# Linear attention and two feed-forward layers: a step's matmuls regrouped by array shape, scores of two heads in turn, decay tables pair by pair

## The chip, the cores and the metric

One core of a Trainium2 chip runs the whole kernel. The metric is the device time of one execution in microseconds (us). TensorE (PE; its weight loads are PEld), VectorE (DVE), ScalarE (ACT) and GpSimd (POOL) work beside each other; SyncE (SP) issues the loads. An engine works through its instructions in the order in which the program issues them, and waits on semaphores for what other engines make.

## The reference

Three layers in a row, all float32:

```python
# attention: q, k, v (4, 8, 768, 64), lam (8,); blocks of 64
for b in range(nb):
    intra = einsum('bhic,bhjc->bhij', qb, kb) * Dmask      # lam ** (i - j), i >= j
    intra = einsum('bhij,bhjd->bhid', intra, vb)
    inter = einsum('bhid,bhde->bhie', qb * lam_pow, kv_state)
    out[:, :, sl] = intra + inter
    kv_state = lam_block * kv_state + einsum('bhsd,bhse->bhde', kb * rev_pow, vb)
# soft mixture of 8 experts on x = out as (3072, 512)
logits = x @ phi                                            # 32 slots
slot_input = softmax(logits, axis=0).T @ x
slot_out[e] = relu(slot_input[e] @ w1[e]) @ w2[e]
x = softmax(logits, axis=1) @ slot_out
# feed-forward: 512 -> 2048 -> 512
h = x @ w_in
return (h * sigmoid(1.702 * h)) @ w_out                     # w_in, w_out stored as float64
```

## The kernel before, in words

The kernel works in blocks of 128 positions (chunks), not 64. A half sequence of one batch (384 positions, R = 3 chunks) is a group `g`, of which there are NG = 8; a group has NHP = 4 pairs of heads. One group and one pair is a step `s`, so there are NSTEP = 32. Two heads of 64 columns lie side by side in 128 partitions.

A step's work is cut into functions, and a loop written out by hand (L524 to L597) runs them for several steps at once: iteration `i` runs the scores of step i+1, the transposes of step i+2, the output of step i and the output transposes of step i-1. This order is the order of the instructions on every engine; nothing reorders it. The parts:

- `load_step` (L111): loads of q, k and v by SP into rotating buffers; a load waits until its buffer is free.
- `do_q` (L240): ScalarE turns the loaded q into the order by chunks.
- `do_T` (L247): TensorE transposes q and k (128x128, three chunks each), ScalarE copies them out as qT and kT.
- `do_SC` (L283): scores, k against q, one head after the other, three chunks each. A head uses 64 rows of the array, the other head the other 64, and each has its PSUM bank ("s0", "s1"). VectorE multiplies each head's scores with its decay table `dec` into AT. With `between`, which step 0 uses, the transposes of step 1 stand between the heads.
- `do_kd` (L275): ScalarE scales k by the decay to the end of the chunk. `do_qd` (L269): GpSimd scales qT.
- `do_ST` (L299): per chunk and head one 128x64 matmul of kd and v into bank "st", then VectorE updates the states (two instructions of 64x64 per chunk).
- `do_X` (L320): the output of a step in bank "x": the state part (one 128x128 matmul per chunk, L328; the very first chunk of a sequence has none) and the attention part, v against AT (128x64, per chunk and head; L332 for the very first chunk, L337 for the others). ScalarE copies it out as xT.
- `do_XT` (L342): three 128x128 transposes of xT into bank "xt", copied out by ScalarE as x in natural order.

Every four steps a group's tail runs, in pieces spread over iterations by `ph` = i mod 4: `tail_logits` (128x32 matmuls with phi, bank "m"), `tail_L` (transposes, then reductions on VectorE), `tail_max` (running maximum), `tail_exp` (the maximum broadcast by a small matmul on 32 rows, then exponentials), and one group later `tail_slot`, `tail_acc`, `tail_z` (128x32 matmuls of the exponentials with x into bank "xt" and with ones into bank "m"; VectorE adds both up).

An fp32 matmul appears in the trace as two records, a transpose as one.

Ahead of the loop VectorE makes the eight decay tables (`make_dec`, L492, a scan of 128x128 per head) and the powers `qtab`. Weights of the experts come in 64 pieces of 512 KB (`load_pieces`, `load_piece`), 33 of them during the steps, nine as the attention's rooms come free, the rest as experts free theirs; ten float64 pieces of w_in and w_out are loaded and converted early as well. After the steps come the last group's tail, the experts (L775 on) and the feed-forward part (L1049 on).

Of the kernel before, what the change touches and what calls it, by code (L numbers as in the profile page):

```python
# [17 lines left out]
def attention_moe_gelu_kernel(  # L18
# [16 lines left out]
    B, H, S, D = q.shape  # L35
# [44 lines left out]
    def bank(tag, name):  # L80
        return psp.tile([P, 512], F32, tag=tag, name=name)
# [149 lines left out]
    def state(s, c):  # L231

        b, hf, hp, g = step_of(s)
        if c == R:
            return S_3[hp]
        return S_a[2 * (s % 2) + (c - 1 if c < R else c - R - 1)]
# [10 lines left out]
    def do_T(s):  # L247
        b, hf, hp, g = step_of(s)
        qt, kt = q_t[s], k_t[s]
        bq = bank("tq", "bq")  # L250
        bk = bank("tk", "bk")
        for c in range(R):
            PE.transpose(bq[:, c * P:(c + 1) * P], qt[:, c].rearrange("p h d -> p (h d)"), ident)  # L253
        for c in range(R):
            PE.transpose(bk[:, c * P:(c + 1) * P], kt[:, c].rearrange("p h d -> p (h d)"), ident)  # L255
        def room(tag, elsewhere):
            if elsewhere:
                return tailp.tile([P, HS], F32, tag="xT", name=tag, bufs=NHP + 1)
            return early.tile([P, HS], F32, tag=tag, name=tag, bufs=1)


        t = room("qT", s in (1, NSTEP - 1))
        ACT.activation(out=t.rearrange("m (p c) -> m c p", c=R), in_=bq[:, :HS].rearrange("m (c p) -> m c p", c=R),  # L263
                       func=AF.Copy)
        tk = room("kT", s == 1)
        ACT.activation(out=tk, in_=bk[:, :HS], func=AF.Copy)
        qT[s], kT[s] = t, tk
# [12 lines left out]
                           scale=dec[:, 2 * hp + h, P - 1:P])  # L280
        kd[s] = t

    def do_SC(s, between=None):  # L283
        b, hf, hp, g = step_of(s)
        bs = [bank(f"s{h}", "bs") for h in range(2)]
        for h in range(2):
            if h == 1 and between:
                between()
            hs = slice(h * D, (h + 1) * D)
            for c in range(R):  # L290
                cs = slice(c * P, (c + 1) * P)
                PE.matmul(bs[h][:, cs], kT[s][hs, cs], qT[s][hs, cs], start=True, stop=True)  # L292
        for h in range(2):
            t = attn.tile([P, R, P], F32, tag=f"AT{h}", name="AT")
            DVE.tensor_tensor(out=t, in0=bs[h][:, :HS].rearrange("m (c i) -> m c i", c=R),  # L295
                              in1=dec[:, 2 * hp + h, None, :].to_broadcast([P, R, P]), op=ALU.mult)
            AT[s, h] = t
# [19 lines left out]
                                             scalar=qtab[r, hp, P - 1:P], in1=src,  # L317
                                             op0=ALU.mult, op1=ALU.add)

    def do_X(s):  # L320
        b, hf, hp, g = step_of(s)
        bx = bank("x", "bx")


        first = hf * R
        for c in range(R):
            if first + c > 0:
                PE.matmul(bx[:, c * P:(c + 1) * P], state(s, first + c), qdT[s][:, c, :],  # L328
                          start=(first > 0 and c == 0), stop=False)
            else:  # L330
                for h in range(2):
                    PE.matmul(bx[h * D:(h + 1) * D, 0:P], v_t[s][:, 0, h, :], AT[s, h][:, 0, :],  # L332
                              start=True, stop=False)
        for c in range(R):
            if first + c > 0:
                for h in range(2):
                    PE.matmul(bx[h * D:(h + 1) * D, c * P:(c + 1) * P], v_t[s][:, c, h, :],  # L337
                              AT[s, h][:, c, :], start=False, stop=(c == R - 1))
        xT[s] = tailp.tile([P, HS], F32, tag="xT", name="xT", bufs=NHP + 1)
        ACT.activation(out=xT[s], in_=bx[:, :HS], func=AF.Copy)  # L340

# [71 lines left out]

    def tail_exp(g, tag="m", between=None, room="e"):
        bb = bank(tag, "bb")
        PE.matmul(bb[:, :NS], mr[g % 2][:NS].to_broadcast([NS, P]), ident[:NS, :NS], start=True, stop=True)
        a = tailp.tile([P, R, NS], F32, tag="a", name="a", bufs=1)
        DVE.tensor_tensor(out=a, in0=tl["L", g], in1=bb[:, None, :NS].to_broadcast([P, R, NS]), op=ALU.subtract)
        if between:
            between()  # L420
        e = tailp.tile([P, R, NS], F32, tag=room, name="e", bufs=1)
        ACT.activation(out=e, in_=a, func=AF.Exp)
        if g > 0:
            ACT.activation(out=tl["al", g], in_=tl["md", g], func=AF.Exp)
        tl["e", g] = e
# [46 lines left out]
    with tc.manual_schedule():  # L472
# [7 lines left out]
        def warm_up(n):  # L480
            for _ in range(n):
                PE.matmul(bwarm, warm[:, :P], warm, start=True, stop=True)
# [9 lines left out]
        def make_dec(h):  # L492

            DVE.tensor_tensor_scan(out=dec[:, h], data0=lam_b[:, h:h + 1].to_broadcast([P, P]), data1=ident,
                                   initial=0.0, op0=ALU.mult, op1=ALU.add)
# [5 lines left out]
        while n < P:  # L501
            DVE.tensor_tensor(out=qtab[:, :, n:2 * n], in0=qtab[:, :, 0:n],
                              in1=qtab[:, :, n - 1:n].to_broadcast([P, NHP, n]), op=ALU.mult)
            n *= 2
        for h in range(2, H):
            make_dec(h)
        load_step(1, "v")
        load_step(2, "q")
        for t in S_a + S_3:
# [3 lines left out]
        def make_isum():  # L513
            for j in range(G):
                for i in range(G):
                    POOL.tensor_copy(out=isum4[i * NS:(i + 1) * NS, j, :],
                                     in_=ident[i * NS:(i + 1) * NS, i * NS:(i + 1) * NS])
# [6 lines left out]
        for i in range(-2, NSTEP):  # L524
            g, ph = divmod(i, NHP)
            if i > -2:
                load_step(i + 4, "q")
            if i == 1:
                make_isum()
            if 0 <= i + 1 < NSTEP:  # L530

                do_SC(i + 1, (lambda: do_T(1)) if i == -1 else None)
            if 0 <= i + 2 < NSTEP:
                if i != -1:
                    do_T(i + 2)
                if i == -2:
                    warm_up(1)
                do_q(i + 3)
            if ph == 0 and 0 <= g - 2 < NG:
                tail_slot(g - 2)  # L540
                tail_acc(g - 2)
                tail_z(g - 2)
            if ph == 2 and 0 <= g - 1 < NG and i < NSTEP - 2:
                tail_max(g - 1)
            if ph == 3 and 0 <= g - 1 < NG:
                tail_exp(g - 1)
            if 0 <= i + 1 < NSTEP:
                do_ST(i + 1)
            if 0 <= i + 2 < NSTEP:
                do_kd(i + 2)  # L550
            if 0 <= i < NSTEP:
                if i == NSTEP - 1:
                    tail_logits_first(NG - 1)
                if i == NSTEP - 2:
                    tail_max(g - 1)
                do_X(i)
            if i == NSTEP - 4:
                load_pieces(i + 1)
            if i >= 0:
                load_step(i + 3, "v")  # L560
            if 0 <= i + 2 < NSTEP:
                do_qd(i + 2)
            load_step(i + 4, "k")
            if i == -2:
                load_step(2, "v")
                SP.dma_start(out=phi_sb, in_=phi.rearrange("(k p) s -> p k s", p=P))
            load_pieces(i)
            if 0 <= i - 1 < NSTEP:
                do_XT(i - 1)
            c, turn = divmod(i - 2, EVERY)  # L570
            if turn == 0 and 0 <= c < len(EARLY):
                do_early(c)
            if turn == 0 and 0 <= c + 1 < len(EARLY):
                load_early(c + 1)
            if ph == 0 and 0 <= g - 1 < NG:
                tail_logits(g - 1)
            if ph == 1 and 0 <= g - 1 < NG:
                tail_L(g - 1)
            if ph == 3 and 0 <= g - 1 < NG and i < NSTEP - 1:
                tail_row(g - 1)  # L580
            if ph == 0 and 0 <= g - 2 < NG:
                tail_row_exp(g - 2)
            if i == NSTEP - 2:
                early_cm.__exit__(None, None, None)
                slotb_cm = tc.tile_pool(name="slotb", bufs=NPC_B, side="right", reuse_waits="tile")
                slotb = slotb_cm.__enter__()

                rooms = [piece_room(NPC + j) for j in reversed(range(NPC_B))]
                while rooms:
                    load_piece(rooms.pop())  # L590
            if i == NSTEP - 1:
                attn_cm.__exit__(None, None, None)
                slotc_cm = tc.tile_pool(name="slotc", bufs=NPC_C, side="left", reuse_waits="tile")
                slotc = slotc_cm.__enter__()
                for _ in range(NPC_C):
                    load_piece()
# [495 lines left out]
```

## Time and profile before

| what | value |
|---|---|
| time, median of 3 runs | 526.29 us (526.19 to 527.05) |
| the profiled execution | 527.16 us, of which the span of instructions is 525.1 us |
| PE / PEld busy | 510.4 us (97%) / 390.5 us (74%) |
| DVE / ACT / POOL busy | 273.6 (52%) / 276.9 (53%) / 62.5 us (12%) |
| mean granted TensorE clock | 0.996 |
| moved by DMA | 76.18 MB |

The span has three parts: the attention steps up to about 171 us, the last tail and the experts up to about 214 us, and the feed-forward part. A matmul's record lasts longer than the distance to the next, since matmuls are pipelined; what a group costs is therefore read from its first start to the first start of the next group. "128*64" after an operation is the part of the array in rows and columns. The DMA share is the time that packets took, summed, over 16 engines; packets on one engine overlap a little, so it can pass 1.

### The profile page before, as it was taken

To read this page: it belongs to the slowest core of one execution; us is meant where nothing else is said; L and a number is where in the kernel's file an instruction comes from. 1 tells how busy PE (TensorE), PEld (TensorE's weight loads), DVE (VectorE), ACT (ScalarE), POOL (GpSimd) and SP (SyncE) were. 2 spreads that over 40 slices of the span, in tenths; PEclk is the share of its full clock that TensorE was granted. 3 is DMA by queue.
4 is the path that set the end of the run, shared out by engine and by line. 5 is a ranking of instruction groups with operands and counts; after the bars stand their busy time and mean duration, and the time that the engine had idled before them with its cause. 6 is when DMAs were issued, how large, how long until landed. Compare 5 with 4: busy or idle time off the path is not lost.

```text
span 525.1 us, 9470 instructions
## 1 busy us (share of the span) xinstructions
PE 510.4 (97%) x3561; PEld 390.5 (74%) x3561; DVE 273.6 (52%) x613; ACT 276.9 (53%) x566; POOL 62.5 (12%) x110
## 2 busy tenths in 40 slices
PE   7999999999999999999889899999999999999997
PEld 4778778778777643667667588888888888888886
DVE  6667867776665411599999883222422221322222
ACT  4676767676664433778666565333333333533332
POOL 3443344232221100000000000000000000000000
PEclk9899999999999999999999999999999999999999
DMA  7598898899789899545434302000110000300003
GB/s 169 147 266 260 239 268 257 242 257 257 212 240 330 294 394 390 208 149 170 159 123 160 122 0 84 37 1 0 60 61 0 1 0 1 121 1 0 1 0 120
DMA packets 82748, 76.18 MB, mean 145 GB/s; under 512 B 54288, under 2 KB 62736, under 8 KB 82704
## 3 DMA queue, kind: packets, MB, share of 16 engines
q1 hardware_dynamic: 82672, 75.58, 45.9%
q8 instruction: 28, 0.46, 0.4%
q14 instruction: 16, 0.13, 0.1%
q0 software_dynamic: 32, 0.00, 0.0%
HBM read 69.28 MB, written 6.29 MB: 144 GB/s over the span
## 4 chain that ended last, share of the span: by engine, by line
PE 81%; DVE 12%; DMA 3%; issue 2%; ACT 2%; DVEq 0%; ACTq 0%; POOLq 0%
PE bo L971 40%; PE bs L292 7%; PE bx L328 4%; PE bx L337 4%; PE bhh L924 3%; PE bt L348 3%; PE bq L253 3%; PE bst L305 3%; PE bh L731 2%; DMA w<-in_moe_w_dram 2%; PE bacc L753 2%; PE bk L255 2%; DVE glo L938 2%; PE bp L430 1%; PE bl L358 1%
## 5 line engine op out<-in xcount | busy, mean ns | idle before, releaser
L971 PE MATMUL bo<-wlo,ghi 128*128 128x512 f32 x382 | 150.2, 395 | 2.6 <-DVE wlo L769 2.5
L971 PE MATMUL bo<-whi,glo 128*128 128x512 f32 x382 | 149.9, 394 | 0.0
L971 PE MATMUL bo<-whi,ghi 128*128 128x512 f32 x382 | 148.9, 391 | 0.1
L938 DVE TENSOR_TENSOR glo<-g,ghi 128x768 fp32r<-128x768 f32 x64 | 61.2, 956 | 146.1 <-ACT ghi L935 146.1
L932 ACT ACTIVATE g<-bhh 128x384 f32<-128x384 f32 x128 | 56.0, 488 | 122.6 <-PE bhh L924 119.6
L971 PEld LDWEIGHTS bo<-wlo,ghi 128*128 128x128 f32 x382 | 71.7, 188 | 20.2 <-DVE wlo L769 4.3
L971 PEld LDWEIGHTS bo<-whi,glo 128*128 128x128 f32 x382 | 71.7, 188 | 15.5 <-DVE glo L938 0.3
L971 PEld LDWEIGHTS bo<-whi,ghi 128*128 128x128 f32 x382 | 71.7, 188 | 14.3 <-DVE W2s L883 0.5
L935 ACT ACTIVATE ghi<-g 128x768 fp32r<-128x768 f32 (+1 forms) x65 | 54.4, 836 | 2.1
L292 PE MATMUL bs<-qT,kT 64*128 64x128 f32 x384 | 41.4, 290 | 2.5 <-DVE AT L295 2.1
L292 PEld LDWEIGHTS bs<-qT,kT 64*128 64x128 f32 x384 | 35.0, 188 | 11.4 <-issue 4.6
L263 ACT ACTIVATE qT<-bq 128x384 f32<-128x384 f32 x32 | 22.6, 706 | 38.1 <-PE bq L253 38.1
L272 POOL TENSOR_TENSOR qdT<-qT,qtab 128x384 f32<-128x384 f32 x32 | 32.2, 1006 | 85.5 <-PE bx L328 35.4
L295 DVE TENSOR_TENSOR AT<-bs,dec 128x384 f32<-128x384 f32 x64 | 32.6, 551 | 13.8 <-PE bs L292 13.5
L924 PE MATMUL bhh<-cT,W2s 128*128 128x384 f32 x128 | 33.7, 340 | 4.8 <-DVE W2s L883 2.7
L924 PEld LDWEIGHTS bhh<-cT,W2s 128*128 128x128 f32 x128 | 23.9, 188 | 11.5 <-DVE W2s L883 3.5
L279 ACT ACTIVATE kd<-k,dec 128x192 f32<-128x192 f32 x64 | 25.3, 444 | 1.7 <-ACT q L244 1.4
L337 PE MATMUL bx<-AT,v 128*64 128x128 f32 x320 | 24.5, 283 | 0.0
L340 ACT ACTIVATE xT<-bx 128x384 f32<-128x384 f32 x32 | 15.6, 487 | 12.2 <-PE bx L337 11.5
L328 PE MATMUL bx<-qdT,sa 128*128 128x128 f32 x128 | 21.1, 288 | 0.0
L244 ACT ACTIVATE q<-qr 128x384 f32<-128x384 f32 x32 | 16.5, 515 | 7.0 <-DMA qr<-in_q_dram 6.8
L174 ACT ACTIVATE cvm<-f 128x512 f32<-128x512 f32 x27 | 17.7, 670 | 4.2 <-DMA f<-in_moe_w_in_dram 2.8
(174 smaller groups left out, 607.7 us busy)
## 6 DMA issues: line engine op xcount, KB each, us to landing
w<-in_moe_w_dram SPq DMA_DIRECT2D x64, 512.0 KB, 5.9
f<-in_moe_w_out_dram SPq DMA_DIRECT2D x15, 512.0 KB, 4.8
qr<-in_q_dram SPq DMA_DIRECT2D x32, 192.0 KB, 4.6
k<-in_k_dram SPq DMA_DIRECT2D x64, 96.0 KB, 3.3
v<-in_v_dram SPq DMA_DIRECT2D x64, 96.0 KB, 3.3
f<-in_moe_w_in_dram SPq DMA_DIRECT2D x12, 512.0 KB, 4.1
out_dram<-o SPq DMA_DIRECT2D x23, 256.0 KB, 2.1
stage<-in_moe_w_in_dram SPq DMA_DIRECT2D x8, 256.0 KB, 4.5
```

The costliest lines, as they stand in the source:

```text
L263: ACT.activation(out=t.rearrange("m (p c) -> m c p", c=R), in_=bq[:, :HS].rearrange("m (c p) -> m c p", c=R), func=AF.Copy)
L272: POOL.tensor_tensor(out=qdT[s], in0=qT[s].rearrange("m (c i) -> m c i", c=R), in1=qtab[:, hp, None, :].to_broadcast([P, R, P]), op=ALU.mult)
L279: ACT.activation(out=t[:, :, h, :], in_=k_t[s][:, :, h, :], func=AF.Copy, scale=dec[:, 2 * hp + h, P - 1:P])
L292: PE.matmul(bs[h][:, cs], kT[s][hs, cs], qT[s][hs, cs], start=True, stop=True)
L295: DVE.tensor_tensor(out=t, in0=bs[h][:, :HS].rearrange("m (c i) -> m c i", c=R), in1=dec[:, 2 * hp + h, None, :].to_broadcast([P, R, P]), ...
L328: PE.matmul(bx[:, c * P:(c + 1) * P], state(s, first + c), qdT[s][:, c, :], start=(first > 0 and c == 0), stop=False)
L337: PE.matmul(bx[h * D:(h + 1) * D, c * P:(c + 1) * P], v_t[s][:, c, h, :], AT[s, h][:, c, :], start=False, stop=(c == R - 1))
L924: PE.matmul(bh[j][u][:, :HS], W2s[:, f * P:(f + 1) * P], cT[tg // (NTG // 2)][:, t0:t0 + HS], start=True, stop=True)
L932: ACT.activation(out=g[j][:, u * HS:(u + 1) * HS], in_=bh[j][u][:, :HS], func=AF.Gelu_apprx_sigmoid)
L935: ACT.activation(out=ghi[j][:, o], in_=g[j][:, o], func=AF.Copy)
L938: DVE.tensor_tensor(out=glo[j][:, o], in0=g[j][:, o], in1=ghi[j][:, o].bitcast(F32), op=ALU.subtract)
L971: PE.matmul(ob[t], a[j][:, t * P:(t + 1) * P], w[f], start=(begin and i == 0), stop=(end and i == 2))
```

## The change

`do_SC` issues the scores chunk by chunk with the two heads in turn, and no longer takes other work between the heads. `do_X` is split: `do_XS` issues the state part for all chunks that have one, `do_XA` the attention part for all chunks and the copy. `tail_exp`'s broadcast uses all 128 rows. `make_dec` makes two tables ahead of the loop and two more in each of the iterations -1, 0 and 1, behind the scores. The order within an iteration becomes: scores of i+1, [tables], transposes of i+2, output transposes of i-1, `do_q`, `tail_L`, `tail_max`, `tail_exp`, state part of i; then state matmuls of i+1, `do_kd`, attention part of i; then `tail_slot`, `tail_acc`, `tail_z`, `tail_logits`; then the loads and the rest as before.

```diff
-    def do_SC(s, between=None):
+    def do_SC(s):
         bs = [bank(f"s{h}", "bs") for h in range(2)]
-        for h in range(2):
-            if h == 1 and between:
-                between()
-            hs = slice(h * D, (h + 1) * D)
-            for c in range(R):
-                cs = slice(c * P, (c + 1) * P)
+        for c in range(R):
+            cs = slice(c * P, (c + 1) * P)
+            for h in range(2):
+                hs = slice(h * D, (h + 1) * D)
                 PE.matmul(bs[h][:, cs], kT[s][hs, cs], qT[s][hs, cs], start=True, stop=True)
...
-    def do_X(s):
+    def do_XS(s):
-        bx = bank("x", "bx")
+        bx = bxs[s] = bank("x", "bx")
         first = hf * R
+        chunks = [c for c in range(R) if first + c > 0]
+        for c in chunks:
+            PE.matmul(bx[:, c * P:(c + 1) * P], state(s, first + c), qdT[s][:, c, :],
+                      start=(c == chunks[0]), stop=False)
+
+    def do_XA(s):
+        bx = bxs.pop(s)
         for c in range(R):
...
+            for h in range(2):
+                PE.matmul(bx[h * D:(h + 1) * D, c * P:(c + 1) * P], v_t[s][:, c, h, :],
+                          AT[s, h][:, c, :], start=False, stop=(c == R - 1))
         xT[s] = tailp.tile([P, HS], F32, tag="xT", name="xT", bufs=NHP + 1)
         ACT.activation(out=xT[s], in_=bx[:, :HS], func=AF.Copy)
...
     def tail_exp(g, tag="m", between=None, room="e"):
-        PE.matmul(bb[:, :NS], mr[g % 2][:NS].to_broadcast([NS, P]), ident[:NS, :NS], start=True, stop=True)
+        PE.matmul(bb[:, :NS], mr[g % 2].to_broadcast([P, P]), ident[:, :NS], start=True, stop=True)
...
-        for h in range(2, H):
-            make_dec(h)
...
             if 0 <= i + 1 < NSTEP:
-                do_SC(i + 1, (lambda: do_T(1)) if i == -1 else None)
+                do_SC(i + 1)
+            if 0 < i + 2 < NHP:
+                for h in range(2):
+                    make_dec(2 * (i + 2) + h)
             if 0 <= i + 2 < NSTEP:
-                if i != -1:
-                    do_T(i + 2)
+                do_T(i + 2)
                 if i == -2:
                     warm_up(1)
+            if 0 <= i - 1 < NSTEP:
+                do_XT(i - 1)
+            if 0 <= i + 3 < NSTEP:
                 do_q(i + 3)
-            if ph == 0 and 0 <= g - 2 < NG:
-                tail_slot(g - 2)
-                tail_acc(g - 2)
-                tail_z(g - 2)
-            if ph == 2 and 0 <= g - 1 < NG and i < NSTEP - 2:
+            if ph == 1 and 0 <= g - 1 < NG:
+                tail_L(g - 1)
+            if ph == 2 and 0 <= g - 1 < NG:
                 tail_max(g - 1)
             if ph == 3 and 0 <= g - 1 < NG:
                 tail_exp(g - 1)
+            if i == NSTEP - 1:
+                tail_logits_first(NG - 1)
+            if 0 <= i < NSTEP:
+                do_XS(i)
             if 0 <= i + 1 < NSTEP:
                 do_ST(i + 1)
             if 0 <= i + 2 < NSTEP:
                 do_kd(i + 2)
             if 0 <= i < NSTEP:
-                if i == NSTEP - 1:
-                    tail_logits_first(NG - 1)
-                if i == NSTEP - 2:
-                    tail_max(g - 1)
-                do_X(i)
+                do_XA(i)
+            if ph == 0 and 0 <= g - 2 < NG:
+                tail_slot(g - 2)
+                tail_acc(g - 2)
+                tail_z(g - 2)
+            if ph == 0 and 0 <= g - 1 < NG:
+                tail_logits(g - 1)
...
-            if 0 <= i - 1 < NSTEP:
-                do_XT(i - 1)
...
-            if ph == 0 and 0 <= g - 1 < NG:
-                tail_logits(g - 1)
-            if ph == 1 and 0 <= g - 1 < NG:
-                tail_L(g - 1)
```

## Rows read from the trace of the kernel before

**Rows 1.** By stretch: length; PE, PEld, DVE, ACT, POOL busy; granted clock; DMA share; GB/s.
```profile
12.00:17.31 5.31, 5.31 (x46) 4.17 (x46) 3.93 (x15) 2.28 (x5) 0.37 (x1) 0.68 0.35 91
17.31:158.66 141.35, 141.35 (x1508) 108.55 (x1506) 99.16 (x294) 95.42 (x229) 51.65 (x76) 1.00 0.88 247
...
186.00:212.00 26.00, 26.00 (x298) 9.76 (x290) 3.96 (x18) 9.11 (x21) 1.49 (x5) 1.00 1.04 396
```

**Rows 2.** Waits of TensorE's weight loads, 17.31 to 158.66: total, times, longest.
```profile
PEld bz L445 <- issue: 3.7, 12, 0.3
```

**Rows 3.** TensorE in order of time, one step: start, length, line, output<-inputs, count.
```profile
104.30 0.57 PE L305 MATMUL bst<-v,kd 128*64 128x64 f32 x12
104.70 0.39 PE L332 MATMUL bx<-AT,v 128*64 128x128 f32 x4
105.02 0.71 PE L328 MATMUL bx<-qdT,sa 128*128 128x128 f32 x4
105.66 0.66 PE L337 MATMUL bx<-AT,v 128*64 128x128 f32 x8
106.25 0.55 PE L348 MATMUL bt<-ident,xT 128*128 128x128 f32 x3
106.73 1.26 PE L292 MATMUL bs<-qT,kT 64*128 64x128 f32 x12
107.92 0.55 PE L253 MATMUL bq<-ident,q 128*128 128x128 f32 x3
```

**Rows 4.** TensorE in order of time, last tail.
```profile
171.25 0.83 PE L393 MATMUL bL<-phi_sb,xT 128*128 128x32 f32 x6
171.92 0.53 PE L348 MATMUL bt<-ident,xT 128*128 128x128 f32 x3
```

**Rows 5.** TensorE in order of time, a second half step.
```profile
156.59 0.88 PE L337 MATMUL bx<-AT,v 128*64 128x128 f32 x12
157.40 0.55 PE L348 MATMUL bt<-ident,xT 128*128 128x128 f32 x3
```

**Rows 6.** TensorE in order of time, slots (with tail_z behind) to the state matmuls.
```profile
93.21 1.06 PE L430 MATMUL bp<-xn,e 128*32 128x512 f32 x6
...
94.23 0.57 PE L305 MATMUL bst<-v,kd 128*64 128x64 f32 x12
```

**Rows 7.** VectorE in order of time, the same step.
```profile
94.39 0.74 DVE L439 SCALAR_TENSOR_TENSOR acc<-acc,al,bp 96x512 f32<-96x512 f32 x1 [1.19 <-PE bz L445]
95.06 0.21 DVE L450 SCALAR_TENSOR_TENSOR zsum<-zsum,al,bz 96x1 f32<-96x1 f32 x1
...
95.68 0.59 DVE L316 SCALAR_TENSOR_TENSOR sa<-sa,qtab,bst 64x64 f32<-64x64 f32 x2
```

**Rows 8.** All engines in order of time, the start (SPq: SP issues a load).
```profile
7.61 0.90 SPq L124 DMA_DIRECT2D k<-in_k_dram  x2
7.64 3.55 DVE L494 TENSOR_TENSOR_SCAN dec<-lam_b,ident 128x128 f32<-128x128 f32 x6
...
8.52 0.49 ACT L266 ACTIVATE kT<-bk 128x384 f32<-128x384 f32 x1
...
11.11 0.99 DVE L295 TENSOR_TENSOR AT<-bs,dec 128x384 f32<-128x384 f32 x2
...
11.78 1.67 PE L292 MATMUL bs<-qT,kT 64*128 64x128 f32 x12 [2.14 <-DVE AT L295]
...
17.31 1.26 PE L292 MATMUL bs<-qT,kT 64*128 64x128 f32 x12
```

**Rows 9.** DMA issues: KB each, median us from issue to landing.
```profile
w<-in_moe_w_dram SPq DMA_DIRECT2D x64, 512.0 KB, 5.9
...
k<-in_k_dram SPq DMA_DIRECT2D x64, 96.0 KB, 3.3
```

**Rows 10.** TensorE's weight loads in order of time, end of the experts.
```profile
212.65 0.14 PEld L753 LDWEIGHTS bacc<-w,hz 128*32 128x32 f32 x4 [1.18 <-DMA w<-in_moe_w_dram]
```

**Rows 11.** Waits of SP's issues, 17.31 to 158.66.
```profile
SPq L124 <- PE bx L337: 38.5, 26, 5.1
```

More of the change, by code (lines that the diff above doesn't have):

```diff
@@ L318, in do_ST @@
                                              op0=ALU.mult, op1=ALU.add)
-    def do_X(s):
+    bxs = {}
+    def do_XS(s):
         b, hf, hp, g = step_of(s)
-        bx = bank("x", "bx")
+        bx = bxs[s] = bank("x", "bx")
         first = hf * R
-        for c in range(R):
[L327 to L338, printed above, removed]
+        chunks = [c for c in range(R) if first + c > 0]
[4 more added lines that the diff above has]
+        bx = bxs.pop(s)
+        for c in range(R):
+            for h in range(2):
+                PE.matmul(bx[h * D:(h + 1) * D, c * P:(c + 1) * P], v_t[s][:, c, h, :],
+                          AT[s, h][:, c, :], start=False, stop=(c == R - 1))
         xT[s] = tailp.tile([P, HS], F32, tag="xT", name="xT", bufs=NHP + 1)
```

## The prediction

> **What bounds the kernel now.** I read the stretches first. From 17.31 to 158.66 us lie 28 of the 32 attention steps, 5.05 us each. There TensorE is marked busy for all 141.35 us at the full 2.4 GHz (granted 1.00), while VectorE has 99 us of work and ScalarE 95, and the DMA engines are 0.88 occupied [rows 1]. Busy is not proof, so the waits come second: TensorE's weight loads wait for other engines or data hardly at all; the longest sum in that stretch is 3.7 us, marked "issue", and no DMA stands in it [rows 2]. So attention is a queue of matmuls in program order, and what one group costs is read from its start to the start of the next.
>
> That is the third view, TensorE's rows of one step [rows 3]. Scores 106.73 to 107.92 = 1.19 us for 12 records; state update 0.40 for 12; first-chunk attention 0.32 for 4; state part of the output 0.64 for 4; the other attention matmuls 0.59 for 8; output transposes 0.48 for 3. These prices aren't proportional to the counts. Six full-array matmul records that are followed by transposes take 0.67, 0.112 each, with no gap [rows 4]. Three transposes between two other kinds cost 0.48, not 3 x 0.112 = 0.34. The 0.15 over is what leaving one shape of array and entering another costs. A first half step changes shape six times: scores (64 rows), transposes (128x128), state and attention (128x64), state part (128x128), attention (128x64), output transposes (128x128).
>
> **The change, part by part.**
>
> *Bunching.* Three changes of shape are left: scores, then all 128x128 work, then all 128x64 work. The output transposes behind the input ones: 0.48 becomes 3 x 0.11 = 0.33, saves 0.15. The state part behind them: 0.64 becomes 4 x 0.112 = 0.45, saves 0.19 (that transposes and matmuls mix without loss is the 171.25 row, read in the other direction [rows 4]). Attention in one piece: 12 records take 0.81 where 8 take 0.59, so four more cost 0.22 [rows 3, 5]. State update, first chunk and eight more in one go are 0.40 + 0.32 + 2 x 0.22 = 1.16 in place of 0.40 + 0.32 + 0.59 = 1.31, saves 0.15. Together 0.49.
>
> *Scores in turn.* The two heads use different row halves and different PSUM banks. At 0.112 a record, 12 in a row would take 1.34 and an entry and exit 0.15 to 0.2; they take 1.19, so the heads overlap in part already, in the middle. In turn, they can overlap throughout: 6 x 0.112 + 0.2 = 0.87, saves 0.32. That is the near end, since 128x64 work alternates its two column halves and gets 12 records into 0.40 [rows 3]. The far end is nothing saved (no more overlap than now); I take 0.32. The Trainium skill (TensorE: Matmul & The Clock Gate, Measured speedup vs the span model) has four row tiles reach 3.07x, not 4x; an estimate by that share, 1.54x for two, makes the group 1.0 us and saves 0.2. No run here shows row tiles alone, and the sum keeps 0.32.
>
> One step so saves 0.49 + 0.32 = 0.81, and 28 steps 22.7 us. The maximum's broadcast, now on 128 rows (7 times), and the 128x32 tail matmuls, now together (6 times), save a change of shape each: 13 x 0.15 = 2.0. Against it:
>
> *A new wait in every fourth step.* tail_z and tail_logits share bank "m". Before, a whole half step lies between them; now logits stand directly behind, and must wait until VectorE has read tail_z's result. VectorE now first does the state updates of the same step. Count from the state matmuls' start: they end at 0.6, six updates of about 0.29 take VectorE to 2.35; TensorE is through with attention at 1.16 and with slots and tail_z (1.02 [rows 6]) at 2.2; accumulation 0.74 and sum 0.21 [rows 7] end at about 3.4. Logits could have begun at 2.3: a gap of 1.1, in six steps (steps 8 to 28) 6.6 us. Behind the waiting matmul stand the next scores, so all of TensorE waits. Bounds 0 (VectorE ahead) and 1.5 (also late); I take 1.1.
>
> TensorE's sum for the 28 steps: 141.35 - 22.7 - 2.0 + 6.6 = 123.3 us, 4.4 a step. ScalarE's 95 and VectorE's 99 us, plus the tables, fit into it.
>
> *What is late next: the DMA engines.* Their work in these steps does not change: 0.88 x 141.35 = 124.4 us of occupancy. The highest share that this trace holds for long is 1.04, in the expert stage (packets overlap, so it passes 1) [rows 1]. The bounds are therefore 119.6 us (1.04 reached) and 141.35 (0.88 stays, no gain). TensorE's floor and the DMA's now lie together, and loads are issued step by step, so neither is reached: I take a share of 0.98, nearer to the row of the saturated stage since the queue will rarely run dry: 127.0 us. The steps save 14.3 us.
>
> *Decay tables pair by pair.* VectorE makes six tables from 7.64 to 11.19 before the first mask product at 11.11 [rows 8]; the second scores wait for it, to 11.78, after which TensorE runs at a mean granted 0.68, between 1.2 and 2.4 GHz, through 17.31 [rows 1, 8]. Afterwards the first mask products can begin at 7.7, and the scores of step 1 when its kT is there, at 9.0 [rows 8]. Step 2's transposes then wait for k: the second half issued at about 8.1 [rows 8], landing 3.3 later [rows 9] at 11.4. From there 0.33 rest of the transposes, 0.45 + 0.2 state part, 1.16 attention: scores of step 2 at about 13.6 in place of 17.31. That is 3.7 if the clock stays up; the tables still cost 1.2 us in each of three steps on VectorE, which then stands at some 5 us a step and trails TensorE slightly. I take 3.5 (bounds 1.5, with the idle gap and low clock still there, and 4.5).
>
> *The rest.* The last three steps save about 2 (two full bunchings and one with fewer matmuls). Then the experts: their last weight load already waits 1.18 us for DMA [rows 10], and the DMA engines are full there. An attention stage that leaves a longer queue pushes that out; its cover, the partly empty stretch before 186 us, is small. I subtract 1.5 (0 to 4). The feed-forward part keeps its order and its time.
>
> Sum: 14.3 + 3.5 + 2 - 1.5 = 18.3 us. The profiled execution took 527.16 (span 525.1 and 2.1 around it), 0.87 above the median of 526.29; I take the sum from the median: 508.0 us.
>
> **Rivals.**
>
> A. *The DMA sets the pace.* Loads are issued when buffers come free, one step's at a time, so the share stays at 0.88 to 0.94 and attention takes 132 to 141 us: 0 to 9 saved, with the start and the end 4 to 13: 513 to 522, middle 517. For it: the share is already high while TensorE waits for nothing. Against: nothing shows TensorE or ScalarE waiting on it now, and SP waits for the output matmuls before it issues v, 38.5 us in 26 steps [rows 11], idle time that a shorter step takes away.
>
> B. *TensorE's sum is reached in full*, without the gap at bank "m": 141.35 - 24.7 = 116.7, so the DMA's 119.6 rules: 21.8 + 3.5 + 2 - 1 = 26: 500. Against: it needs the expert stage's share with small rows (96 KB loads) in the queue.
>
> C. *Scores gain nothing.* 28 x 0.32 = 9 us less: TensorE 132.2 us, saves 9.1 + 3.5 + 2 - 1 = 13.6: 512.7. It lies within the range.
>
> D. *Slower: the k load comes late.* v waits for the output matmuls [rows 11], and k follows it. These matmuls now end a step instead of standing before the output transposes, so v is issued as the next scores begin; with some 0.5 an issue [rows 8] the second k goes out 1.6 us into the step, and its transposes come 1.2 us into the one after. A step must then last at least the landing + 0.4. At the present 3.3 that is 3.7, no bound. With the queue full, k may land like w, 5.9 [rows 9]. It decides from 4.85: steps of 5.25, 28 x 0.2 = 5.6, eat up start and end. At 5.0 steps take 5.4, +9.8 - 5.5 = +4.3: 530.6. Against: a longer step empties the queue again.
>
> **How the numbers follow.** Forecast 0.53 (502 to 514), A 0.23, B 0.10, C 0.07, D 0.04, and 0.03 for no change (A at its worst with 3.5 us lost at the start or in the experts). About 0.2% (1 us) is what a measurement of this kernel tells from none. A, B and C are all faster, as is the forecast: 0.93; same 0.03; slower 0.04. The range reaches into B's upper and A's lower half: 501 to 518, leaving out half of B, a third of A, and D.
>
> **What would show it.** Right: scores' start to next start at about 0.87; one change of shape between the input transposes and the state matmuls; first mask product near 7.7 us; 28 steps in about 127 us with a DMA share near 0.98; a gap before logits behind VectorE's zsum in every fourth step. Wrong: scores still at 1.19 (C); DMA share below 0.94 and TensorE waiting for q or k (A, D); the experts' last pieces waiting more than 4 us for DMA; no gap at logits (B).

## The result, and the profile after

The changed kernel takes 512.12 us (511.51 to 512.19, 4 runs) against 526.67 us (526.19 to 527.5, 4 runs) on the same chip: a ratio of 0.972, with a 95% interval of 0.9703 to 0.9736. It is faster by 14.6 us. Forecast were 18.3 us less (508.0 us, range 501 to 518).

The span went from 525.1 to 510.2 us, 14.9 less, and the places can be read off. The scores of step 2 begin at 13.46 us (17.31 before, [rows 8]): 3.85 won at the start. From there to the scores of step 30 it takes 132.25 us (141.35 before, [rows 1]): 9.1 won. From the scores of step 30 to the first matmul behind the experts it takes 53.0 us (55.0): 2.0 won. The feed-forward part takes 311.5 us in both.

The stretches of the changed kernel, columns as in [rows 1]:

```profile
8.00:13.46 5.46, 4.69 (x64) 3.72 (x62) 5.27 (x14) 3.35 (x7) 3.38 (x4) 1.00 0.70 160
...
13.46:145.71 132.25, 120.91 (x1508) 97.72 (x1507) 101.02 (x303) 93.71 (x232) 51.09 (x75) 1.00 0.95 265
...
172.00:198.00 26.00, 26.00 (x300) 9.99 (x294) 4.04 (x18) 9.11 (x21) 1.49 (x5) 1.00 1.04 396
```

TensorE is no longer busy all the time in the 28 steps: 120.9 of 132.25 us. The DMA share rose from 0.88 to 0.95, and the start keeps the full clock (1.00, where 12.00 to 17.31 us had 0.68).

TensorE in order of time, the last step of a group with its tail, and the step behind it:

```profile
81.31 0.94 PE L291 MATMUL bs<-qT,kT 64*128 64x128 f32 x12
82.18 0.55 PE L253 MATMUL bq<-ident,q 128*128 128x128 f32 x3
82.94 0.52 PE L255 MATMUL bk<-ident,k 128*128 128x128 f32 x3 [0.22 <-DMA k<-in_k_dram]
83.29 0.49 PE L349 MATMUL bt<-ident,xT 128*128 128x128 f32 x3
83.62 0.61 PE L330 MATMUL bx<-qdT,sa 128*128 128x128 f32 x4
84.16 0.57 PE L304 MATMUL bst<-v,kd 128*64 128x64 f32 x12
84.56 0.83 PE L338 MATMUL bx<-AT,v 128*64 128x128 f32 x12
85.32 1.06 PE L431 MATMUL bp<-xn,e 128*32 128x512 f32 x6
86.20 0.21 PE L446 MATMUL bz<-ones,e 128*32 128x1 f32 x6
87.46 0.85 PE L359 MATMUL bl<-xT,phi_sb 128*32 128x384 f32 x8 [1.04 <-DVE zsum L451]
88.24 0.94 PE L291 MATMUL bs<-qT,kT 64*128 64x128 f32 x12
89.11 0.55 PE L253 MATMUL bq<-ident,q 128*128 128x128 f32 x3
89.49 0.49 PE L255 MATMUL bk<-ident,k 128*128 128x128 f32 x3
89.82 0.49 PE L349 MATMUL bt<-ident,xT 128*128 128x128 f32 x3
```

Start to next start again: scores 0.87 (1.19 in [rows 3]), output transposes 0.33 (0.48), state part 0.54 (0.64), state matmuls and attention 0.40 + 0.76 = 1.16 (1.31). Two waits are new. From q's transposes to k's it is 0.38 where k is there (89.11 to 89.49) and more where it isn't (82.18 to 82.94): the excess over 0.38, added up over the 28 steps, is 6.9 us. And logits stand 1.26 behind tail_z (86.20 to 87.46). In the kernel before, the work behind tail_z stood 0.14 behind it (94.09 to the 94.23 of [rows 6]):

```profile
94.09 0.21 PE L445 MATMUL bz<-ones,e 128*32 128x1 f32 x6
```

So 1.1 is lost, six times, 6.5 us in all (1.0 to 1.12 each). VectorE shows why, in the step of the changed kernel shown above:

```profile
84.78 0.48 DVE L313 COPY sa<-bst 64x64 f32<-64x64 f32 x2 [0.95 <-PE bst L304]
85.29 0.59 DVE L315 SCALAR_TENSOR_TENSOR sa<-sa,qtab,bst 64x64 f32<-64x64 f32 x2
85.91 0.59 DVE L315 SCALAR_TENSOR_TENSOR s<-sa,qtab,bst 64x64 f32<-64x64 f32 x2
86.53 0.74 DVE L440 SCALAR_TENSOR_TENSOR acc<-acc,al,bp 96x512 f32<-96x512 f32 x1
87.20 0.20 DVE L451 SCALAR_TENSOR_TENSOR zsum<-zsum,al,bz 96x1 f32<-96x1 f32 x1
```

The state updates come first; zsum, which frees bank "m", ends at 87.40, and logits begin at 87.46. The waits of the 28 steps (total, times, longest):

```profile
ACT q L244 <- DMA qr<-in_q_dram: 19.4, 17, 2.6
PEld bk L255 <- PE bq L253: 7.2, 11, 1.2
...
PE bl L359 <- DVE zsum L451: 5.1, 5, 1.0
PE bk L255 <- DMA k<-in_k_dram: 4.8, 10, 0.9
```

The "PEld bk" line is put down to q's transposes, but there is no such wait in the kernel before, where k is there in time: it is the wait for k again, seen at the weight loads. ScalarE waits for q more than TensorE for k, but with little direct effect on TensorE: "bq" behind ScalarE is late by 0.5 us in all.

The start, engines mixed, against [rows 8]:

```profile
7.82 0.90 SPq L124 DMA_DIRECT2D k<-in_k_dram  x2
7.88 1.01 DVE L294 TENSOR_TENSOR AT<-bs,dec 128x384 f32<-128x384 f32 x2
...
8.82 1.67 DVE L495 TENSOR_TENSOR_SCAN dec<-lam_b,ident 128x128 f32<-128x128 f32 x2
9.30 0.94 PE L291 MATMUL bs<-qT,kT 64*128 64x128 f32 x12 [0.31 <-ACT kT L266]
```

The experts' last weight load, against [rows 10], waits 0.31 instead of 1.18:

```profile
197.74 0.14 PEld L759 LDWEIGHTS bacc<-w,hz 128*32 128x32 f32 x4 [0.31 <-DMA w<-in_moe_w_dram]
```

### The profile page after: what moved, and what is told of

The parts are those of the page before. It is cut to its first block, busy times and chain, and to the rows that moved or that the text cites. A ratio compares the mean times of both kernels' runs of the same rounds, so it can differ in the third digit from the quotient of the medians.

```text
span 510.2 us, 9441 instructions
## 1 busy us (share of the span) xinstructions
PE 486.4 (95%) x3561; PEld 377.9 (74%) x3561; DVE 272.5 (53%) x613; ACT 273.6 (54%) x566; POOL 62.9 (12%) x110
## 4 chain that ended last, share of the span: by engine, by line
PE 67%; DMA 11%; DVE 11%; ACT 4%; issue 3%; SPq 3%; ACTq 0%; DVEq 0%
PE bo L977 42%; DMA k<-in_k_dram 5%; DMA qr<-in_q_dram 5%; PE bhh L930 4%; PE bacc L759 3%; PE bh L737 3%; SPq L124 2%; PE bx L338 2%; PE bx L330 2%; DVE glo L944 2%; PE bs L291 2%; PE bk L255 1%; PE bst L304 1%; PE bt L349 1%; DVE wlo L775 1%
## 5 line engine op out<-in xcount | busy, mean ns | idle before, releaser
L291 PEld LDWEIGHTS bs<-qT,kT 64*128 64x128 f32 x384 | 23.9, 187 | 9.5 <-issue 6.3
L291 PE MATMUL bs<-qT,kT 64*128 64x128 f32 x384 | 30.0, 289 | 0.7 <-ACT kT L266 0.7
L338 PE MATMUL bx<-AT,v 128*64 128x128 f32 x384 | 26.6, 273 | 0.0
L255 PE MATMUL bk<-ident,k 128*128 128x128 f32 x96 | 16.4, 281 | 5.5 <-DMA k<-in_k_dram 5.4
L338 PEld LDWEIGHTS bx<-AT,v 128*64 128x64 f32 x384 | 20.6, 137 | 0.1
L330 PE MATMUL bx<-qdT,sa 128*128 128x128 f32 x128 | 19.8, 277 | 0.0
```

## Experiments

The theory: TensorE's queue of matmuls was and is the bound, and what the forecast missed is the wait for k. The main rival: after the change the DMA engines set the length of a step, so that further time taken from TensorE turns into waiting. "Steps" below are the 28 from the scores of step 2 to those of step 30; "waits for k" is the excess over 0.38 from q's transposes to k's in them.

### Parts alone

**Tables alone**, on the kernel before:

```diff
-        for h in range(2, H):
-            make_dec(h)
...
                 do_SC(i + 1, (lambda: do_T(1)) if i == -1 else None)
+            if 0 < i + 2 < NHP:
+                for h in range(2):
+                    make_dec(2 * (i + 2) + h)
```

> The kernel before with the decay tables alone made pair by pair. Theory (VectorE's six tables held the second scores up): first mask product near 7.7 us, scores of step 2 some 2 to 3.5 us earlier than 17.31, total 523 to 524.5. Rival (the early start came from the new order of the first steps, and without it the loads of step 2 hold TensorE anyway): less than 1 us, 525.5 to 526.5.

Measured: 523.6 us (before 526.49; ratio 0.9941, 0.992 to 0.9962). The scores of step 2 begin at 14.42, 2.9 us earlier; the steps take 141.36 as before; the clock stays up from the start on:

```profile
8.00:14.42 6.42, 5.96 (x70) 4.82 (x68) 5.10 (x17) 3.75 (x9) 2.33 (x3) 1.00 0.72 168
```

So the tables make three quarters of the 3.85 us, and bunching the first steps the rest (the changed kernel with scores head by head, below, has both, and its scores of step 2 begin at 13.43).

**Scores in turn alone**, on the kernel before (the transposes of step 1 go behind the scores of step 0):

```diff
-        for h in range(2):
-            if h == 1 and between:
-                between()
-            hs = slice(h * D, (h + 1) * D)
-            for c in range(R):
-                cs = slice(c * P, (c + 1) * P)
+        for c in range(R):
+            cs = slice(c * P, (c + 1) * P)
+            for h in range(2):
+                hs = slice(h * D, (h + 1) * D)
                 PE.matmul(bs[h][:, cs], kT[s][hs, cs], qT[s][hs, cs], start=True, stop=True)
```

> The kernel before with the scores of two heads in turn alone. Theory (TensorE's matmul queue is the bound): scores' group 0.87 in place of 1.19 us, 31 x 0.32 = 10 us less, some 1 lost to late loads: 517 to 518. Rival (the DMA engines set the step's length): the group shortens but the time goes into waits for q or k: 522 to 526.

Measured: 518.58 us (0.9855, 0.9826 to 0.9883), 7.9 less than before; steps 134.00, the group 0.87:

```profile
102.35 0.94 PE L290 MATMUL bs<-qT,kT 64*128 64x128 f32 x12
103.22 0.55 PE L253 MATMUL bq<-ident,q 128*128 128x128 f32 x3
```

Of 28 x 0.32 = 9.0 us in the steps 7.35 arrive; waits for k take 1.2. A little above what the theory gave, well away from the rival.

**The changed kernel with scores head by head** (the loops of the edit above turned back):

> The changed kernel with the scores head by head again. Theory (TensorE is the bound, k loads come late only because the steps are short): scores' group back to 1.19, +10 us, of which the 7 us of waits for k give back 3 to 6: 516 to 519. Rival (DMA bound): at most +2: 512 to 514, with the waits for k all but gone.

Measured: 516.3 us (0.9807, 0.9773 to 0.9841). The steps grow by 3.4 to 135.63, not by 9: waits for k fall from 6.9 to 2.1. So bunching and tables are worth some 10 us together, and the scores in turn, worth 8 by themselves, add 4 on top. Most of the rest is lost to late k loads, 4.8 us of them.

### The wait of logits

**Logits ahead of the slots:**

```diff
+            if ph == 0 and 0 <= g - 1 < NG:
+                tail_logits(g - 1)
             if ph == 0 and 0 <= g - 2 < NG:
                 tail_slot(g - 2)
...
-            if ph == 0 and 0 <= g - 1 < NG:
-                tail_logits(g - 1)
```

> The changed kernel with the logits ahead of the slots, so that they no longer wait for VectorE to read tail_z's result out of the same bank. Theory: six gaps of 1.1 us go, -6.7, of which later k loads take back up to 3: 505.5 to 508.5. Rival (the DMA engines already set the pace): -0 to -1.5, 510.5 to 512, the waits for k longer by as much as the gaps were.

Measured: 511.59 us (0.9723, 0.9692 to 0.9753), the changed kernel's time. It does not speak for the rival, though: bank "m" is still shared, and now tail_z waits for ScalarE to copy the logits out, which stands behind a late q:

```profile
PEld bz L446 <- ACT lp L362: 10.1, 6, 3.5
```

One wait in place of the other, so the test settles nothing.

**tail_z in another bank**, logits in their place:

```diff
-                tail_z(g - 2)
+                tail_z(g - 2, "tk")
```

> The changed kernel with tail_z in the bank of the k transposes, so that logits, still in their place behind it, have bank m to themselves and wait for neither VectorE nor ScalarE's copy. Theory (TensorE's waits add up, k comes late by itself): logits' 6.6 us of waits go, the waits for k grow from 6.9 to 8 to 10: 507 to 509. Rival (the DMA engines set the steps' length, the gap only moved): at most -1, 511 to 512.5, waits for k and q up by 5 or more.

Measured: 508.07 us (505.2 to 510.32; 0.965, 0.9597 to 0.9704). The gap is gone, the steps take 126.42, 5.8 us less, and waits for k are 5.5:

```profile
13.51:139.93 126.42, 120.85 (x1507) 97.31 (x1507) 100.57 (x302) 93.30 (x232) 50.66 (x75) 1.00 0.99 274
```

The rival had the gap move elsewhere; the DMA share rose to 0.99 instead. The four runs lie 5 us apart, for a reason that nothing here shows, and the trace is of one at 506.32. The same change on the kernel with a third buffer for k, below, confirms it: 508.94 to 503.38 us, with runs about 1 us apart, and 5.5 us less in the steps.

### The wait for k

**k ahead of v:**

```diff
+            load_step(i + 4, "k")
             if i >= 0:
                 load_step(i + 3, "v")
...
-            load_step(i + 4, "k")
```

> The changed kernel with the k load issued ahead of the v load, which waits for the end of the output matmuls. Theory (k comes late because its issue stands behind v's): TensorE's waits for k fall from 6.9 to under 2, 506 to 508. Rival (k comes late because the DMA engines are full): the wait goes over to v or q, 510.5 to 512.5.

Measured: 517.25 us (0.9809, 0.9775 to 0.9842): slower than the changed kernel, which neither side had expected. The trace is of the fastest of the four runs, 514.57, and has steps of 134.43, 2.2 longer. Waits for k do fall, to 1.3, but the k issue needs a free buffer, which ScalarE frees with kd, behind the q copy: in one step kd ends at 99.00 and k is issued at 99.03. SP, waiting there, holds up v, pieces and the next q. Its waits (from 13.46 to 134 us; the profile names the copy that overlaps kd's end), and ScalarE's (in the 28 steps):

```profile
SPq L124 <- ACT xT L341: 35.1, 25, 2.4
...
ACT q L244 <- DMA qr<-in_q_dram: 33.4, 24, 3.5
```

In the changed kernel SP waits for ScalarE there for some 7 us, and ScalarE for q for 19.4: there too a late q makes some k loads late. The DMA share fell to 0.93.

**Both of the last two:**

> Both: tail_z in another bank and k ahead of v. If TensorE is the bound: both waits gone, steps near 118 to 121 us, 500 to 503. If the DMA engines are: their share goes to 1.0 and above and the steps stay at 126 or more, 506 to 511.

Measured: 514.26 us (0.976, 0.9718 to 0.9802), steps 132.01 at a share of 0.93: the logits' gap is won and the loop over ScalarE and SP loses it again, with q's transposes late by 6.2 us in all and waits for k of 4.0. Not a DMA limit, since the engines have more idle time than with the bank alone.

**Half as many pieces up to step 26:**

```diff
-            n = min(NPC, i * NPC // (NSTEP - 2), NPC - 1 if i < NSTEP - 5 else NPC)
+            n = i * NPC // (2 * (NSTEP - 2)) if i < NSTEP - 5 else NPC
```

> The changed kernel with half as many expert pieces loaded up to step 26, and the rest in one go behind. If full DMA engines make k and q late: up to the scores of step 26 no wait for k or q is left, steps of 4.45 us on average as the matmuls and the logits' gap add up, 4.45 x 24 = 107 us from the scores of step 2 to those of step 26 (112.9 now). If it is the order of issue: the waits for k stay at 5 to 7 us. The total is expected to be longer than 520, since the late pieces then hold up the last steps and the experts.

Measured (total 532.69 us, as the late pieces come in the way): from the scores of step 2 to those of step 26 it takes 110.85, against 113.81 in the changed kernel (not the 112.9 of the expectation), at a DMA share of 0.82 instead of 0.96.

```profile
13.62:124.47 110.85, 103.33 (x1292) 84.29 (x1291) 87.56 (x263) 80.11 (x200) 46.18 (x69) 1.00 0.82 215
```

Waits for k fall from 6.4 to 2.6 in this stretch, not to none, so neither side's figure holds. A fuller DMA queue makes more than half of them, and the rest fits the order: even with a landing of 3.4 us (median of this run; 3.8 in the changed kernel) a step must last that and 0.4 more, 3.8 us, for the load to land in time, and the short ones last 3.7.

**A third buffer for k, ahead of v**, so that the issue waits for nothing (one piece buffer fewer makes the room):

```diff
-    NPC = 33
+    NPC = 32
...
-        for src, nm, ts, bufs, pool in ((k, "k", k_t, 2, early), (v, "v", v_t, 3, attn)):
+        for src, nm, ts, bufs, pool in ((k, "k", k_t, 3, early), (v, "v", v_t, 3, attn)):
...
+            load_step(i + 4, "k")
             if i >= 0:
                 load_step(i + 3, "v")
```

> The changed kernel with a third buffer for k (paid for with one of the 33 piece buffers) and the k load ahead of the v load, where it now waits for nothing. Theory (k is late because a short step gives its load less than its landing and 0.4 us; without the hold on SP that undid the test with two buffers): waits for k under 1.5 us, steps 126 to 128, 506 to 509. Rival (the DMA engines set the pace and any load may be the late one): waits for q take over, steps 131 to 133, 511 to 513.

Measured: 508.94 us (0.9662, 0.9645 to 0.9679). No wait for k is left, though the DMA share rose; the steps take 128.03, 4.2 less. The rest of the 6.9 us comes back as small waits elsewhere, 1.2 of them at q's transposes:

```profile
13.57:141.60 128.03, 120.47 (x1508) 98.79 (x1507) 101.40 (x303) 92.39 (x231) 50.88 (x75) 1.00 0.98 269
```

**The same with tail_z in bank "tk":**

> The same with tail_z in the bank of the k transposes. Theory: both waits gone, DMA share at 1.02 or more, steps 120 to 123 us, 501 to 504. Rival (DMA bound): steps 125 to 127, 506 to 509, as with the bank alone.

Measured: 503.38 us (0.955, 0.9531 to 0.9569), steps 122.54, some 4 us above the matmuls' own sum of about 118 (worked out further down), at a DMA share of 1.00 (the theory's 1.02 was not needed).

**tail_z in "tk" and the third buffer for q instead** (`bufs=3` for "qr", k in its old place, `NPC = 32`):

> tail_z in the other bank and a third buffer for q in place of one for k. If late q loads, through ScalarE's queue, are what holds k's release and so SP: waits for q fall below 8 us, those for k to 3, steps 122 to 124, 503 to 506. If k alone matters: as with the bank alone, 507 to 509.

Measured: 506.94 us (0.9629, 0.961 to 0.9648), steps 125.46, with waits for k of 7.1: a buffer for q alone does about nothing over the bank alone. Since this kernel, too, has one piece buffer fewer, that is not what the third buffer for k gains by.

**Third buffers for both, k ahead of v, tail_z in "tk":**

> tail_z in the other bank, third buffers for both k and q, k ahead of v. If only latency of loads is left: no waits for k or q, steps at the matmuls' own sum of 118 to 119 us, 499 to 501. If the DMA engines bind: share 1.03 to 1.05, steps 120 to 124 with waits left, 501 to 506.

Measured: 502.97 us (501.48 to 504.14; 0.9547, 0.9524 to 0.9571), the fastest kernel beside the one with tail_z in "tk" and a third buffer for k alone (503.38), from which it can't be told apart in total.

```profile
13.51:133.98 120.47, 119.13 (x1507) 97.90 (x1506) 100.15 (x302) 91.97 (x231) 50.52 (x75) 1.00 1.03 282
```

The steps are down to 120.47 with a share of 1.03, next to the 1.04 of the expert stage. Here TensorE's sum of about 118 and what the DMA engines need (120.47 x 1.03 / 1.04 = 119.3, an estimate) lie close together, and neither leaves much to gain. Logits no longer wait for tail_z:

```profile
80.56 1.06 PE L431 MATMUL bp<-xn,e 128*32 128x512 f32 x6
81.44 0.18 PE L446 MATMUL bz<-ones,e 128*32 128x1 f32 x3
81.46 0.51 PE L359 MATMUL bl<-xT,phi_sb 128*32 128x384 f32 x1
81.47 0.18 PE L446 MATMUL bz<-ones,e 128*32 128x1 f32 x3
81.50 0.83 PE L359 MATMUL bl<-xT,phi_sb 128*32 128x384 f32 x7
82.25 0.94 PE L291 MATMUL bs<-qT,kT 64*128 64x128 f32 x12
```

## Why the prediction was right, and where it was off

**Bunching** was right in kind and nearly in size. Output transposes saved 0.15 and attention 0.15 as forecast. The state part saved 0.10, not 0.19: it now stands last in the 128x128 bunch and still pays the way out, which the working left out (0.09 x 28 = 2.5 us). The broadcast on 128 rows saved 0.19 each time (forecast 0.15). **Scores in turn** saved the 0.32 forecast; the two row halves do overlap throughout, and the near end of the bounds held, not the 0.2 of the lower estimate beside it.

**The logits' wait** was forecast at 1.1 us, six times, 6.6 in all, and measured at 6.5, by the mechanism named; with another bank the steps became 5.8 us shorter. The 132.25 us less the two waits (6.9 and 6.5) and 0.5 for q are about 118; TensorE's forecast sum of 123.3 without its 6.6 is 116.7.

**"What is late next: the DMA engines"** is the step that failed. It set the steps to 127.0 us by a share of 0.98; they took 132.25 at 0.95, and that the DMA engines can't do more is refuted: three kernels go to 0.99, 1.00 and 1.03 as soon as waits are taken away. Rival A comes out half right: its steps of 132 to 141 us just take in the 132.25, and that a load's issue waits for its buffer is part of the cause, as the third buffer for k shows; but the logits' wait, which A doesn't have, is in the 132.25 too. What came in place of the share was the mechanism of rival D, the late k load, at a size of 6.9 us instead of a net loss. Its rule, a step of at least the landing + 0.4, fits; it was held against a mean step of 4.4. Hardly a step has that length: three of four last 3.7 to 4.6 and one 5.6 to 7.7. Against a landing of 3.8 us (median of k in the 28 steps) the short ones are too short, and the step behind one waits: the eleven waits for k of more than 0.2 us all stand behind a step of 3.7 to 4.6, none behind a long one.

**The start** was forecast at 3.5 and measured at 3.85; the clock, which was the lower bound's reason, stays up. **The last steps and the experts** were forecast at +2 - 1.5 and gave 2.0, but not by the first term alone. From the scores of step 30 to the last tail it takes 10.9 us (12.0 before), 1.1 less, since one group of output transposes now waits 0.6 for ScalarE's copy; the rest is nearly all the experts', which got 1.0 shorter instead of 1.5 longer. Their last wait for DMA shrank from 1.18 to 0.31; why was not tried, so the sign of this term was wrong for a reason that stays open. Added up: of the 18.3 us forecast, the steps gave 5.2 less (132.25 against 127.0), the start 0.35 more and the end 1.5 more (2.0 against 0.5), which makes the 14.9 us that the span lost. That the total came as near as it did is in part luck: the end's 1.5 us made up for some of what the steps fell short.

## What to carry to other kernels

Read what a group of matmuls costs from its start to the next group's start, beside the same group in other company: what neighbours of another array shape add shows at once, and can be summed. When steps are shortened, hold each load's landing against the shortest step, not the mean one. A wait for a PSUM bank was not removed here by changing the order of its two users, but by giving one of them another bank. A load issued early on an in-order queue gains nothing if its buffer comes free late, and it holds up the loads behind it.

## What the runs showed of the hardware

Two matmul streams on the two row halves run side by side almost fully: 12 records in 0.87 us, where one stream at 0.112 each with entry and exit would need an estimated 1.5. A change of array shape costs 0.1 to 0.15 us (three transposes 0.48 alone and 0.33 in the bunch; three changes fewer saved 0.40 a step). The step from 64 to 32 columns is no cheaper than the one to 64 rows: attention takes 0.76 to the next start before the slots as before scores. Transposes and full matmuls mix at no cost (0.33 for three transposes with the state part behind them). With small rows in the queue (96 KB loads of k and v) the DMA engines hold a share of 1.03 over 120 us, 282 GB/s, against 396 GB/s at 1.04 with 512 KB pieces alone.
